# First layer of batches 4 to 7 in block form, eleven long spin products, no zero fills, a split last PSUM bank, and a new order of all the work

## The chip, the core and the metric

The kernel runs on one core of one Trainium2 chip. The metric is device time in microseconds, from launch to end. The engines are named as the profile names them: PE (matrix products), PEld (its weight loads), DVE and ACT (elementwise work), POOL and SP (here mostly queues that issue transfers); "PEq", "SPq" and so on are an engine's instruction queue.

## What is computed

Attention without softmax, with a squared ReLU, and behind it a two-layer network with an exact GELU. From the reference:

```
scores = scale * np.matmul(q, k.transpose(0, 1, 3, 2))
attn = np.maximum(scores, 0.0) ** 2 / S
out = np.matmul(attn, v)
...
x = attn_out.transpose(0, 2, 1, 3).reshape(B * S, H * D)
h = x @ w_in
g = 0.5 * h * (1.0 + erf(h * inv_sqrt2))
return (g @ w_out).astype(np.float32)
```

q, k and v are 8 batches x 12 heads x 448 positions x 64, w_in is 768 x 2048, w_out is 2048 x 768, all in float32; the products are made in bf16. The output has 3584 rows of 768.

## The kernel before, in words

**Attention.** A batch has three head groups of four heads. A score tile (`add_steps`, L718) is one block of keys of one head group: four products on quarters of PE (L736), a ReLU out of PSUM on ACT (L748) or DVE (L750), a square on DVE (L757). Seven tiles make a head group; then 28 products make its values (`add_av`, L782, L797), which ACT and DVE copy out as xT (L515, L513). Batch 0 works in halves of 224 columns. Scores and values need q and k transposed. For batches 0 and 1 PE does that (`add_tk`, `add_tq`, L607, L635), with the identity that POOL makes (L1321). For batches 2 to 7 DMA transposes do it, issued by SP (`add_T_dma`, L662), three for each head group.

**First layer.** The plain form (`add_f1`, L838) makes one of 16 output tiles of a batch with six products of 448 columns (L849) and a GELU on ACT (L859). The block form (`add_blocks`, L935, `add_block`, L982) splits the weights and the columns of a batch into 2 x 2 blocks and makes the four results from seven block products instead of eight, after Strassen and Winograd: each block product is made of products of 224 columns (L993), 168 of them in a batch. It needs four sums of x (L960), sums of the weights that are made once (`add_wsums`, L918), and it passes its partial results through DVE (additions, L1030) and ACT (copies, L515; GELUs, L1039 and L1046). Before, batches 0 to 4 take the plain form and 5 to 7 the block form. The results stand in a ring of two batches (`h_ring`, L711), so the GELUs of batch b wait until the second layer has read batch b - 2.

**Second layer.** Rows go in 14 groups of 256 (group 0 as two plain tiles, `add_plain`, L1253). A group (`add_group`, L1130) is the same seven-product form: p1, p6, p2, p7, p5, p4, p3, each of eight products of 384 columns (L1166). Its sums of h are made by DVE (L1147), partial results are added by DVE (L1200) or copied (L513, L515), and SP stores the rows (L1127). Products p5 and p3 share the PSUM bank "c". In the last group (13) p3 and the addition behind it are made in a part of 256 columns and one of 128, in that same bank.

**Buffers.** PSUM has three tiles of two banks, "w" (scores, values, block products, the spin), and two single banks, "f" (everything else). Natural q and k have one buffer from batch 2 on, and their transposes two.

**What sets the order.** A planner (`Scheduler`, L182) holds all operations in the order in which the code adds them, 1436 in all. The text `ORDER` (L83) then fixes by hand what is issued when: each word is a letter for the engine (P for PE, A for ACT, D for DVE, G for POOL, S for SP) and the number of an operation in that list; `place` (L353) takes the words one by one. An engine runs its words strictly in that order. Words with Z are zero fills (L1493, L1499): products of zeros of so many columns on PE, whose result nobody reads. There are eight, all in the first four lines of the text. POOL's loads wait in its queue behind gates (`add_gate`, L698, L703): small copies that read a transposed q, so that a load doesn't overwrite what a transpose still reads. Before all that PE runs 45 spin products of 128 columns on zeros (L1333).

Some words, decoded by counting the additions: G0, G1, G3, G4 load k and q (first half) of batch 0's groups 1 and 2, G2 the values of group 0, G7 the second halves of q; G1435 makes the identity; S541 to S543 are the transposes of batch 4's first head group and P600 to P618 its score products; S704 to S706 are those of batch 5's first head group, whose score products begin at P763. In the new text numbers above some 740 shift: the identity is G1469, and batch 5's first score product is P783.

## Time and profile before

Three runs took 370.45, 370.65 and 370.81 us. The profile is of one execution; its page gives its span, from the first to the last instruction, and no time of its own for it.

| | us |
|---|---|
| median of three runs | 370.65 |
| span of the profiled execution | 367.9 |
| median less span (what lies around it) | 2.75 |
| PE busy, 3573 products | 359.3 |
| DVE busy | 285.1 |
| ACT busy | 199.4 |
| POOL busy | 62.9 |

The stages, by the busy time of each engine in stretches of the span (the ends are starts of products on PE):

| stretch, us | what PE does | PE | DVE | ACT |
|---|---|---|---|---|
| 0 to 34.75 | spin, batch 0's attention, its first layer begins | 31.42 | 27.53 | 28.21 |
| 34.75 to 82.04 | batches 0 to 2: attention, first layer of 0 and 1 | 47.29 | 31.82 | 26.84 |
| 82.04 to 145.57 | attention 2 to 4, first layer of 2, groups 1 to 3 | 63.00 | 54.61 | 36.45 |
| 145.57 to 220.47 | attention 4 to 6, first layer of 3, groups 3 to 5 | 74.90 | 64.71 | 50.65 |
| 220.47 to 250.06 | attention 6 and 7, first layer of 4, group 6 | 29.41 | 27.00 | 22.51 |
| 250.06 to 354.08 | block form of 5 to 7, groups 7 to 12 | 103.95 | 74.27 | 34.73 |
| 354.08 to 367.9 | group 13 and the last stores | 9.28 | 5.19 | 0.00 |

To read the profile's lines: a group line names the line of code, engine, operation, what is written and read, and the busy time; a timeline line gives the start, the duration and the number of merged instructions, and in brackets how long the engine sat idle before and what ended that. Products are pipelined: their durations overlap, so what one costs is read from the distance of starts. Times of transfers are from issue to landing.

### The profile page before, as it was taken

The numbers are of one execution on the slowest core, as the hardware profiler recorded it, in microseconds if no ns is written. First come the engines' busy times: TensorE is split into PE (matmuls) and PEld (weight loads), VectorE is DVE, ScalarE is ACT, GpSimd is POOL, SyncE is SP. The second block draws the span as 40 slices with busy tenths as digits, with TensorE's granted clock in tenths as the row PEclk, the third lists the DMA queues.
The fourth block names the chain that finished last, engine by engine and source line by source line (L and its number), as shares of the span: only waits on it lengthen the run. The fifth ranks groups of instructions, "written<-read, shape, count | busy, mean of one in ns | idle before, by whom it ended". The sixth has DMA issues, their size and how long they took to land.

```text
span 367.9 us, 8474 instructions
## 1 busy us (share of the span) xinstructions
PE 359.3 (98%) x3573; PEld 222.5 (60%) x3573; DVE 285.1 (78%) x473; ACT 199.4 (54%) x319; POOL 62.9 (17%) x103
## 2 busy tenths in 40 slices
PE   7999999999999999999999999999999999999995
PEld 6675654455544455544555544557876897688663
DVE  4998854699788889989598997998788558665862
ACT  5998954536367546765777568863540353045200
POOL 8766304230112140240302000000000000000000
PEclk9999999999999999999999999999999999999998
DMA  9999999999999999999999980002002301210233
GB/s 180 191 202 204 201 178 167 196 201 178 162 218 214 154 186 193 237 214 154 166 110 131 215 183 2 2 2 86 3 0 87 88 0 52 86 37 2 86 87 86
DMA packets 89542, 47.27 MB, mean 128 GB/s; under 512 B 55329, under 2 KB 86049, under 8 KB 89505
## 3 DMA queue, kind: packets, MB, share of 16 engines
q0 software_dynamic: 32912, 22.47, 43.8%
q1 hardware_dynamic: 55952, 23.76, 34.9%
q8 instruction: 28, 0.46, 0.5%
q10 hardware_dynamic: 640, 0.51, 0.4%
q14 instruction: 10, 0.07, 0.1%
HBM read 45.61 MB, written 11.01 MB: 154 GB/s over the span
## 4 chain that ended last, share of the span: by engine, by line
PE 78%; DMA 8%; SPq 5%; DVE 5%; issue 1%; POOL 1%; ACT 1%; DVEq 0%; POOLq 0%; ACTq 0%
PE pso L1166 30%; PE psh L849 19%; PE pb L993 13%; PE ps L736 8%; PE pav L797 7%; SPq L662 5%; DMA wout_sb<-in_moe_w_out_dram 4%; DVE a_sq L757 2%; DMA nq<-in_q_dram 1%; DVE t_sb L1103 1%; DMA qT<-nq 1%; DMA out_dram<-osb 1%; ACT a_sq L748 1%; PE tp L635 1%; DVE part L1030 1%
## 5 line engine op out<-in xcount | busy, mean ns | idle before, releaser
L748 ACT ACTIVATE a_sq<-ps 128x896 bf16<-128x896 f32 (+1 forms) x119 | 104.3, 918 | 36.8 <-PE ps L736 36.6
L757 DVE TENSOR_TENSOR a_sq<-a_sq 128x896 bf16<-128x896 bf16 (+1 forms) x169 | 97.0, 617 | 9.4 <-ACT a_sq L748 8.8
L849 PE MATMUL psh<-xT,win_sb 128*128 128x448 bf16 (+1 forms) x516 | 96.4, 340 | 0.4 <-issue 0.4
L849 PEld LDWEIGHTS <-win_sb 128*128 128x128 bf16 x516 | 48.1, 98 | 45.8 <-issue 9.7
L750 DVE TENSOR_SCALAR a_sq<-ps 128x896 bf16<-128x896 f32 (+1 forms) x50 | 53.5, 1078 | 17.1 <-PE ps L736 17.0
L859 ACT ACTIVATE h_sb<-psh 128x448 bf16<-128x448 f32 x80 | 43.2, 548 | 29.9 <-PE psh L849 29.6
L1166 PEld LDWEIGHTS <-s_sb 128*128 128x128 bf16 x424 | 40.7, 98 | 26.6 <-issue 2.0
L1030 DVE TENSOR_TENSOR part<-pb,part 128x448 f32<-128x448 f32 x60 | 34.6, 620 | 21.5 <-PE pb L993 21.5
L736 PE MATMUL ps<-qT,kT 64*64 64x448 bf16 (+1 forms) x756 | 47.9, 336 | 0.5 <-ACT a_sq L748 0.2
L1166 PEld LDWEIGHTS <-h_sb 128*128 128x128 bf16 x312 | 29.6, 98 | 22.5 <-issue 4.4
L1166 PE MATMUL pso<-wout_sb,s_sb 128*128 128x384 bf16 (+2 forms) x216 | 38.1, 320 | 0.1
L1166 PE MATMUL pso<-wout_sb,h_sb 128*128 128x384 bf16 x208 | 38.1, 326 | 0.0
L1166 PE MATMUL pso<-t_sb,s_sb 128*128 128x384 bf16 x208 | 38.1, 326 | 0.0
L797 PE MATMUL pav<-a_sq,v_sb 64*64 64x448 bf16 (+1 forms) x756 | 36.5, 329 | 0.3 <-issue 0.2
L736 PEld LDWEIGHTS <-kT 64*64 64x64 bf16 x756 | 18.5, 105 | 22.9 <-issue 17.1
L1039 ACT ACTIVATE h_sb<-part 128x448 bf16<-128x448 f32 x36 | 20.1, 578 | 20.2 <-DVE part L1030 19.9
L1200 DVE TENSOR_TENSOR osb<-pso,p_sb 128x384 f32<-128x384 f32 x39 | 21.7, 556 | 11.0 <-PE pso L1166 6.7
L993 PEld LDWEIGHTS <-win_sb 128*128 128x128 bf16 x288 | 27.6, 98 | 2.3 <-issue 0.4
L797 PEld LDWEIGHTS <-v_sb 64*64 64x64 bf16 x756 | 21.2, 107 | 11.7 <-issue 1.3
L703 POOL COPY gate<-qT 128x16 bf16<-128x16 bf16 x15 | 3.7, 246 | 111.0 <-DMA qT<-nq 111.0
L993 PEld LDWEIGHTS <-ws 128*128 128x128 bf16 x216 | 20.7, 98 | 0.0
L1147 DVE TENSOR_TENSOR s_sb<-h_sb 128x1024 bf16<-128x1024 bf16 x26 | 17.8, 685 | 2.3 <-PE pso L1166 2.3
(61 smaller groups left out, 298.4 us busy)
## 6 DMA issues: line engine op xcount, KB each, us to landing
nk<-in_k_dram POOLq DMA_DIRECT2D x23, 224.0 KB, 5.6
nq<-in_q_dram POOLq DMA_DIRECT2D x21, 224.0 KB, 8.3
v_sb<-in_v_dram POOLq DMA_DIRECT2D x5, 672.0 KB, 13.9
out_dram<-osb SPq DMA_DIRECT2D x8, 336.0 KB, 2.9
v_sb<-in_v_dram POOLq DMA_DIRECT2D x9, 224.0 KB, 8.6
out_dram<-osb SPq DMA_DIRECT2D x7, 288.0 KB, 3.2
out_dram<-osb SPq DMA_DIRECT2D x8, 240.0 KB, 3.0
win_sb<-in_moe_w_in_dram POOLq DMA_DIRECT2D x8, 192.0 KB, 8.6
```

Of the source, the lines that this page charges most:

```text
L736: nc.tensor.matmul(ps[64 * j : 64 * j + 64, e, x * w : x * w + w], kT[r, g, i * 128 + 64 * j : i * 128 + 64 * j + 64], moving, start=True, ...
L748: A.activation(ar, ps, AF.Relu, scale=c_att)
L750: V.tensor_scalar(ar, ps, c_att, 0.0, op0=mybir.AluOpType.mult, op1=mybir.AluOpType.max,)
L757: V.tensor_mul(box["a2"][:, :, :used], ar, ar)
L797: nc.tensor.matmul(pav[0][o2 : o2 + 64, e, :w], vt[b][r, 2 * g + e, bass.ts(i, D)], box["a2"][r, y, o : o + w], start=(i == 0), stop=(i == ...
L849: nc.tensor.matmul(ph[:, x * n : x * n + n], win_sb[:, kd, bass.ts(m + x, 128)], xT[b][:, kd, c], start=(kd == 0), stop=(kd == KD - 1),)
L859: A.activation(h_ring()[:, m : m + nm, o + c.start : o + c.stop], box[0][:, :S].rearrange("p (x n) -> p x n", x=nm), AF.Gelu,)
L993: nc.tensor.matmul(bank[name][:, y, z * HS : z * HS + HS], w[:, k, bass.ts(mm, 128)], right()[:, k], start=first and k == 0 and z == 0, st ...
L1030: V.tensor_add(get(to), ps(name), get(other))
L1039: A.activation(h_ring()[:, m : m + 2, o + half[c].start : o + half[c].stop], src().rearrange("p (x n) -> p x n", x=2), AF.Gelu,)
L1166: nc.tensor.matmul(box[bank][:, n0:n1], left()[:, kf], right()[:, kf, n0:n1], start=bool(need) and kf == 0, stop=kf == K2 - 1, skip_group_ ...
L1200: V.tensor_add(out()[:, n0:n1], box[bank][:, n0:n1], other()[:, n0:n1])
```

## The change

The block form starts at batch 4 (`NBLK = 4`): 16 plain first-layer tiles go, 28 block products come, with their sums, passes and GELUs; the buffers of the x sums, and what these sums wait for, shift by one batch. The spin is 11 products of 512 columns. The zero fills are gone. In group 13 the second part of p5 and of p3 (128 columns) goes to a bank of its own, "d", taken from the "w" tiles, and the first addition behind p5 is split as well. Group 6 moves one batch earlier in the code that adds operations, which only matters for numbers, since `ORDER` is new as a whole: it has 1470 words, and stretches of one kind of work, loads, transposes, gates and stores all stand elsewhere. The text below is cut; what is said of the order is counted from the whole of both texts.

```diff
@@ -50,6 +50,7 @@
 DMA_LAT = 2.13
 SWITCH = 0.11
 LEAD = 8
+NBLK = 4
 HALF_M = 6
 PASS_BIAS = -0.4
 SUM_BIAS = -0.3
@@ -77,91 +78,92 @@
 
 COLD_END = 0.0
 K_CUT = 4
-SPIN = 45
+SPIN = 11
 
 
 ORDER = """
-G0 G1 G2 G3 G1435 G4 G5 G6 A10 P11 D13 A16 P17 G7 D12 P14 D18 P42 P39 G8 P19 A15 P21 D43 P33 P36 D44
-A40 D20 Z128 A22 P54 G9 P25 P23 A37 D34 P51 D26 P48 A55 Z1056 D35 A24 P69 D56 Z1024 D41 A49
-P57 Z992 D38 A52 P63 Z448 G117 D70 P45 A58 D53 P66 A64 D50 P27 A46 G118 P31 D59 P60 D28 A67
-G119 D32 A47 P78 P29 D65 G120 A61 P81 Z1088 D68 D30 A79 P93 D62 P108 Z544 D71 A82 P84 Z992
-G121 A94 P75 D109 P72 G122 D83 A85 P90 P129 D80 G123 D73 A76 P105 A74 P102 D95 G124 P131 D130
-A91 P141 D86 A106 D77 P111 P96 D132 A103 P165 P143 D92 A112 D104 D107 A97 P156 D113 P87 G125
-D98 A166 P99 D110 G126 D88 A157 P114 A142 D100 A89 P174 G127 A101 P168 D115 P133 A144 P135
-A116 G128 D175 P171 P159 A169 D134 P251 D136 D170 A160 P145 D158 A172 D167 A252 P162 P186 D176
...
-S541 A465 P467 D462 A518 P470 G413 S542 P519 A516 G414 A459 G415 P521 D471 S543 G416 D472 A520
...
-P654 P594 D653 A646 D659 A655 D650 P596 A647 D667 S710 D595 P660 P766 P663 P672 D597 A661 D767
...
-P1391 D1386 D1390 P1393 D1392 P1395 D1394 P1397 D1405 D1396 P1399 D1403 D1398 S1401 P1407
-D1404 D1400 S1402 P1409 D1406 D1408 P1411 D1410 P1413 D1412 S1423 P1415 D1414 P1417 D1416
-P1419 D1418 S1424 P1420 D1421 S1425 D1422 S1426
+G3 G4 G0 G1 G7 G1469 G122 A10 P11 D13 A16 G117 P17 D12 P14 D18 G2 P42 P23 D15 P25 G6 A43 P36 P33
+P39 G5 D24 P21 D26 P19 G121 A37 P69 D34 P66 G118 A40 D20 D22 P57 A70 P51 G9 D35 P29 P27 A67 D38
+P48 D30 P135 D44 A58 P54 D41 D28 A52 P63 P129 D136 A49 P90 P31 G8 D55 A64 P78 P45 D50 A91 D68
+P96 D32 D46 A79 P93 D47 P105 A97 D53 P81 D59 A94 G120 P111 D56 A106 D71 P75 D65 A82 P72 D98 A112
+P60 D95 A130 D107 G124 P131 D73 A76 D61 P102 A74 P84 A62 D80 P143 D113 D132 A85 G119 P159 D83
+P156 P141 A103 G125 D77 D86 A157 D92 P108 P99 D104 A160 P162 A144 P133 D109 P87 D100 G126 A163
...
+P497 S541 P494 D563 A520 P517 D472 A498 D493 S549 P511 D481 A495 D469 A504 P488 D502 P482 A512
+S546 D489 P615 P618 P521 S547 A483 A518 D484 P535 A619 S544 D616 A522 P606 D496 P600 P609 S545
...
+P660 D622 P566 D565 A623 S704 D659 A661 D656 P630 P666 P568 A628 S389 D567 D638 S707 A631 D635
+P570 A667 D626 A569 S710 D632 P783 D629 P798 P645 D662 S711 D668 A784 D571 P795 P572 S709 D582
...
+P1413 A1362 D1412 A1368 A1402 P1415 A1385 D1414 A1382 P1417 A1357 A1365 D1416 A1348 P1419 D1423
+D1418 P1427 D1424 D1420 S1422 P1429 D1425 S1421 D1428 P1431 D1430 P1433 D1432 P1435 D1434 P1437
+D1426 D1436 P1439 D1443 D1444 D1438 P1456 S1441 P1447 D1440 S1442 D1445 P1449 D1448 P1451 D1446
+D1450 P1453 D1452 S1465 P1455 D1454 P1459 D1457 D1458 P1461 D1460 S1466 P1462 D1463 S1467 D1464
+S1468
 """
 
 
@@ -932,6 +934,8 @@
             s3 = one(3, m0, sub, part(0, 0), part(0, 1), [s1] + done)
             WS[m0] = {1: s1, 2: s2, 3: s3, 4: s4}
 
+    first_blocks = []
+
     def add_blocks(b):
 
 
@@ -946,13 +950,15 @@
         def t(n):
             def fn():
                 if "t" not in box:
-                    tag = "qT" if b == B - 1 else "kT"
+                    tag = "qT" if b == B - 2 else "kT"
                     box["t"] = tpool.tile([128, 4, K1, HS], BF16, tag=tag, name="xs")
                 return box["t"][:, n - 1]
 
             return fn
 
-        gone = [o for (bb, *_), o in QK.items() if bb == (B - 2 if b == B - 3 else B - 1)]
+        gone = [o for (bb, *_), o in QK.items() if bb == (B - 2 if b == B - NBLK else B - 1)]
+        if b == B - 1:
+            gone += first_blocks
 
         def xsum(n, op, l, r, deps):
             return sch.add(
@@ -974,6 +980,8 @@
                 todo.append(add_block(b, m4, y, ms, bank, x, t, TS, xs, old, half))
             for p in zip(*todo):
                 atoms += [(0.58, o) for o in p]
+                if b == B - NBLK:
+                    first_blocks.extend(p)
             for name in ("a", "b", "c"):
                 u, v = bank["end", name]
                 u.joint, v.joint = [v], [u]
@@ -1160,7 +1168,9 @@
 
         def product(bank, left, right, deps, need=(), frees=(), joint=(), n0=0, n1=ND):
             def fn(e):
-                if need:
+                if need and bank == "d":
+                    box[bank] = w_pp.tile([128, 2, NB], F32, tag="w", name="psd")[:, 0]
+                elif need:
                     box[bank] = f_pp.tile([128, NB], F32, tag="f", name="pso")
                 for kf in range(K2):
                     nc.tensor.matmul(
@@ -1220,33 +1230,49 @@
         c11 = passed("a", part(0, left), None, [p2, v2], frees=("f",))
         p7 = product("b", lambda: box["s", 3], lambda: tsum(3), [v2, s3], frees=("s3",))
         v3 = passed("b", part(1, right), first, [p7], need=("osb",))
-        p5 = product("c", lambda: box["s", 1], lambda: tsum(1), [s1, s2], need=("f",), frees=("s1",))
-        c22 = passed("c", part(1, right), part(1, right), [v3, p5])
+        ends = [("c", 0, ND)] if g < NG - 1 else [("c", 0, LAST), ("d", LAST, ND)]
+        p5 = [
+            product(
+                x, lambda: box["s", 1], lambda: tsum(1), [s1, s2],
+                need=("f",) if x == "c" else ("w",), n0=n0, n1=n1,
+            )
+            for x, n0, n1 in ends
+        ]
+        p5[-1].frees = ("s1",)
+        c22 = [
+            passed(x, part(1, right), part(1, right), [v3, o], n0=n0, n1=n1)
+            for o, (x, n0, n1) in zip(p5, ends)
+        ]
         p4 = product("b", lambda: h(1, o2), lambda: tsum(4), [v3])
         c21 = passed("b", part(1, left), first, [p4, v3], frees=("f", "p"))
-        ends = [(0, ND)] if g < NG - 1 else [(0, LAST), (LAST, ND)]
         p3 = [
-            product("c", lambda: box["s", 4], lambda: quad[1, 1], [c22, s4], n0=n0, n1=n1)
-            for n0, n1 in ends
+            product(x, lambda: box["s", 4], lambda: quad[1, 1], [o, s4], n0=n0, n1=n1)
+            for o, (x, n0, n1) in zip(c22, ends)
         ]
         p3[-1].frees = ("s4",)
         c12 = [
-            passed("c", part(0, right), part(0, right), [o], n0=n0, n1=n1)
-            for o, (n0, n1) in zip(p3, ends)
+            passed(x, part(0, right), part(0, right), [o], n0=n0, n1=n1)
+            for o, (x, n0, n1) in zip(p3, ends)
         ]
-        c12[-1].frees = ("f",)
+        c12[0].frees = ("f",)
+        if g == NG - 1:
+            c12[1].frees = ("w",)
         if g < NG - 1:
-            sch.add((("SP", 0.6, 2.8),), store(1, full, [nc.sync] * 2), [c22, c21], frees=("osb",))
+            sch.add((("SP", 0.6, 2.8),), store(1, full, [nc.sync] * 2), c22 + [c21], frees=("osb",))
             sch.add((("SP", 0.6, 2.8),), store(0, full, [nc.sync] * 2), [c11] + c12, frees=("osb",))
         else:
             sch.add((("SP", 0.6, 2.8),), store(0, left, [nc.sync] * 2), [c11])
-            sch.add((("SP", 0.6, 2.8),), store(1, full, [nc.sync] * 2), [c22, c21])
-            for o, (n0, n1) in zip(c12, ends):
+            sch.add((("SP", 0.6, 2.8),), store(1, full, [nc.sync] * 2), c22 + [c21])
+            for o, (_, n0, n1) in zip(c12, ends):
                 c = slice(ND + n0, ND + n1)
                 sch.add((("SP", 0.6, 2.8),), store(0, c, [nc.scalar, nc.sync]), [o])
         for bb in bs:
             readers.setdefault(bb, []).extend(mine)
-        return [(1.3, o) for o in (p1, p6, p2, p7, p5, p4)] + [(1.3 / len(p3), o) for o in p3]
+        split = 1.3 / len(ends)
+        return (
+            [(1.3, o) for o in (p1, p6, p2, p7)] + [(split, o) for o in p5] + [(1.3, p4)]
+            + [(split, o) for o in p3]
+        )
 
     plain = []
 
@@ -1329,8 +1355,9 @@
     A.activation(warm, warm, AF.Gelu)
 
     spin = w_pp.tile([128, 2, NB], F32, tag="w", name="spin")
+    zeros = zero[:, :1].to_broadcast([128, NB])
     for _ in range(SPIN):
-        nc.tensor.matmul(spin[:, 0, :128], zero, zero, start=True, stop=True)
+        nc.tensor.matmul(spin[:, 0, :], zero, zeros, start=True, stop=True)
     ctx.enter_context(tc.manual_schedule())
 
 
@@ -1426,8 +1453,8 @@
         add_load(3, g, g + 1)
     add_v(3, 0, G)
     flow, plans = [], {}
-    F1B = {2: 1, 3: 2, 4: 3, 5: 4}
-    GROUPS = {2: (1,), 3: (2, 3), 4: (4, 5), 5: (6,)}
+    F1B = {2: 1, 3: 2, 4: 3}
+    GROUPS = {2: (1,), 3: (2, 3), 4: (4, 5, 6)}
     for b in range(2, B):
         add_steps(steps(b), dve=True)
         if b == 2:
@@ -1448,7 +1475,7 @@
                     add_load(b + 2, g, g + 1)
                 add_v(b + 2, 0, G)
         flow += [y for g in GROUPS.get(b, ()) for y in add_group(g)]
-    add_wsums(at(B - 1, 1), [F1[B - 4, m, None] for m in range(KF)])
+    add_wsums(at(B - 1, 1), [F1[B - NBLK - 1, m, None] for m in range(KF)])
 
     def woven(x, y):
 
@@ -1460,7 +1487,8 @@
                 out.append(y.pop(0))
         return out + y
 
-    end = woven(add_blocks(B - 3), add_group(7))
+    end = add_blocks(B - 4)
+    end += woven(add_blocks(B - 3), add_group(7))
     end += add_group(8)
     end += woven(add_blocks(B - 2), add_group(9))
     g10 = add_group(10)
```

## The prediction

> **What bounds the kernel now.** I read the page first: which engine is busy, and where.
>
> ```profile
> span 367.9 us, 8474 instructions
> PE 359.3 (98%) x3573; PEld 222.5 (60%) x3573; DVE 285.1 (78%) x473; ACT 199.4 (54%) x319; POOL 62.9 (17%) x103
> PE   7999999999999999999999999999999999999995
> DVE  4998854699788889989598997998788558665862
> DMA  9999999999999999999999980002002301210233
> PE 78%; DMA 8%; SPq 5%; DVE 5%; issue 1%; POOL 1%; ACT 1%; DVEq 0%; POOLq 0%; ACTq 0%
> ```
>
> PE is busy in every slice but the first and last, and it carries 78% of the chain that ended last. A busy PE need not be a PE at work, though, so I went to PE's timeline for what each product costs when nothing holds it: the distance from one start to the next (columns: start, modelled duration).
>
> ```profile
> 53.11 6.98 PE L849 MATMUL psh<-xT,win_sb 128*128 128x448 bf16 x36
> 60.02 0.76 PE L736 MATMUL ps<-qT,kT 64*64 64x448 bf16 x12
> 60.72 3.58 PE L849 MATMUL psh<-xT,win_sb 128*128 128x448 bf16 x18
> 64.23 0.76 PE L736 MATMUL ps<-qT,kT 64*64 64x448 bf16 x12
> ...
> 259.30 1.31 PE L993 MATMUL pb<-xs,win_sb 128*128 128x224 bf16 x12
> 260.45 1.31 PE L993 MATMUL pb<-xT,ws 128*128 128x224 bf16 x12
> 261.60 1.31 PE L993 MATMUL pb<-xT,win_sb 128*128 128x224 bf16 x12
> ```
>
> 36 first-layer products take 60.02-53.11 = 6.91 us, 18 take 64.23-60.72 = 3.51. So one costs (6.91-3.51)/18 = 0.189 us, and 0.11 is left over each time that PE turns from attention to dense products. A block product of 224 columns costs 1.15/12 = 0.0958 us. In the same way three score steps take 0.70 (60.02 to 60.72), and eleven steps of scores and values take 2.21 (111.04 to 113.25): 0.189 a step, and 0.13 for the turn. A second-layer product costs 0.1625 (357.98 to 359.28, eight of them).
>
> With these prices I added up the old order, word by word, and laid the sum beside the timeline. The last product ends at 352.0 in the sum and about 363.4 in the profile. Of the 11.4 us between, 9.6 are there by 34.75 (batch 0's ninth first-layer tile, m = 8): 5.2 before the first transpose, the rest waits of the start, where DVE and ACT are full. In the 329 us after it only 1.8 us are waits: about 0.6 near 99, 0.3 near 102, 0.4 near 250, 0.45 near 275. So after the start PE is the bound, and **PE's sum is the forecast's backbone**.
>
> **The change, part by part.** Sums are made against the profiled execution's span of 367.9 us. The page has no own time for that execution; the median of the runs, 370.65, is 2.75 us longer, and I carry that over.
>
> *Block form of batch 4.* Removed: 96 products x 0.189 = 18.14 us. Added: 168 x 0.0958 = 16.09. **-2.05 us**. [...] The rows above, each product with its own load, show 0.0958, so I go by them.
> DVE gets 20 additions and 4 sums more: from runs of four back to back (2.31 us) and the sums at about 0.45, 20 x 0.58 + 4 x 0.45 = 13.4 us. They lie in the block stage, beside PE: at 250.06 to 354.08 DVE was busy 74 of 104 us (71%). ACT trades 16 GELUs for 16 GELUs and 4 copies.
>
> *The new order.* Counting stretches of one kind on PE (transposes, attention, dense), the old list has 110 and the new one 121: 11 x 0.11 = **+1.2 us**. From batch 0's tile m = 8 to the last product the new list comes to 326.4 us by these prices, the old one to 326.9: most of the block form's gain goes into turns.
>
> *Zero fills.* 6272 columns; at 0.0958 per 224 columns 2.7 us. All lie between 8.46 and 20, where ACT and DVE are full (11 to 20: nearly 9 of 9 us each), so PE waits there anyway: **0**. If the fills did hold up score products, -2.7. If a less busy PE slows, the start's product work between 8 and 20, some 6 us, doubles within 12 us: at most +1.3. The granted clock can't settle it: it says 1.00 even where 45 spin products of 128 columns take 3.8 us (5760 columns, 0.15 us per 224). [...] The longest wait of PE after the spin was 0.86 us (for a load, before 9.72), and fills are 0.2 to 0.6 us each.
>
> *Eleven long products.* 5632 columns against 5760, at the pace of the old ones 3.7 us against 3.8. The first transpose waits for ACT's cast until 5.20 in any case: 0, between -0.1 and +0.2.
>
> *Order of the start.* The identity now stands behind five POOL loads instead of four. One issue is 0.72 to 0.92, so it ends near 5.5 instead of 4.61 and the first transpose starts 0.3 to 0.45 later. Against that, the ACT and DVE work listed ahead of batch 0's tile m = 8, by its rows, sums to 50.3 us on two engines instead of 51.8: -0.7. I take **-0.3**; ends -1.5 and +1.
>
> *Split last bank.* Old tail:
>
> ```profile
> 361.88 1.48 PE L1166 MATMUL pso<-wout_sb,s_sb 128*128 128x256 bf16 x16
> 363.40 0.62 DVE L1200 TENSOR_TENSOR osb<-pso,osb 128x256 f32<-128x256 f32 x2 [0.76 <-PE pso L1166]
> ```
>
> Both additions start after both products, since they share a bank. With two banks the 256-column addition (0.42) runs beside the 128-column product. Eight of these take about 0.55 us of the 1.48, so the first store issues 0.5 earlier and the second behind it. Splitting another product costs 0.02 (1.48 against 1.46). The 128-column half of that product now opens the last group and needs two sums; DVE has 2.6 us for four operations of 0.5 to 0.68, so up to 0.2 late. **-0.5**.
>
> *Moved loads and GELUs.* Batch 0's first value load moves from third to eighth among POOL's loads. By the issue sizes 2.4 MB then land up to and with it; at 183 GB/s to 10 us and 190 after, that is 13 us plus a landing tail of 1 or 2. Its value product moves from behind 10 score tiles (13.74) to behind 12 (about 16): nothing, with about 1 us to spare. At the end batch 7's block form now runs ahead of groups 9 and 10, which still read the ring slot of batch 5, so its 16 GELUs must wait for group 10's last product. From four in 2.26 us and two in 0.98 they take about 8.8 us; PE has one block product and group 11 in between, 9.7 us. Again nothing; without that spare 0.9, group 12 and all behind it would wait, up to 1 us.
>
> *Waits.* The four old ones (1.8 us) stand at places that are all rearranged: -1.8. New ones are unknown: from 0 to the 4.2 of the first rival and 2.4 of the second. I take +1.5, close to what the old order had over the same length.
>
> Sum: -2.05 + 1.2 - 0.3 - 0.5 - 1.8 + 1.5 = -1.95; span 365.95, time **368.7 us** (367.4 to 369.8 if this case holds).
>
> **Rivals.**
> *Transposes come late (slower).* The columns are issue line and microseconds to landing:
>
> ```profile
> qT<-nq SPq DMA_TRANSPOSE x36, 6.4
> kT<-nk SPq DMA_TRANSPOSE x18, 6.8
> ```
>
> Counted in PE work by the prices above, in the old list between 6.9 and 23 us stand between the last transpose of a head group and its first score product, mostly 13 to 18. In the new list it is 6 to 8 for most, 4.4 for batch 4's first group and 4.6 for batch 5's. Against a landing of 6.4 to 6.8 that is a wait of 2.0 to 2.4 on PE at two places, with dense work queued behind the waiting product. Each transpose also waits for a load, which waits in POOL's queue for a gate on earlier transposes: POOL spent 111 us at gates, so lateness is handed on from batch to batch, and all transfers must fit a stage about 17 us shorter. It decides once the waits pass 2 us: with 4.2 in the two places and 1.5 more at batches 6 and 7 the time is 368.7 + 4.2 = **372.9**. Against it: the old order's 6.9 at batch 2 cost PE nothing, and SP often issued up to 5 us before its place in the list.
>
> *DVE becomes the bound of the attention stage (no change).* With 18 us of dense work gone from beside attention, DVE has, from batch 3's first value product to batch 7's second, about 104 us of rows in 117 of PE (89%); the old list 109 in 130 (84%). If DVE manages only 87%, it needs 119.7: 2.4 more, **371.1**. Against it: the old stretch from 220.47 to 250.06 held DVE busy for 27.00 of 29.59 (91%), with about 0.4 of wait.
>
> *The start shrinks by more (faster).* If fills and early waits were in PE's way, up to 2.7 go, and with few new waits the time is 368.7 - 2.2 = **366.5**.
>
> **How the numbers follow.** Forecast 0.47, start shrinks 0.18, DVE bound 0.12, late transposes 0.23. The range leaves out the worst of the late transposes and the best of the start: 366.5 to 372.8. About 0.2% (0.74 us) is what a measurement of this kernel can tell from no change. Faster takes forecast and start (0.65), less 0.02 for its upper edge: 0.63. No change: 0.12; slower: 0.25, with part of the DVE case.
>
> **What the next profile would show.** Block rows for batch 4 at 0.096 each, before the last value product; batch 0's tile m = 8 by 34.5; no PE wait above 0.5 us after it; the last two additions apart, the first beside PE. I am wrong if score products of batches 4 and 5 wait for a transpose, if PE's starts in the attention stage stand further apart than the prices, or if spin, transposes and scores before 20 us run slower than now.

## The result and the profile after

The changed kernel takes **380.63 us** (378.06 to 383.24), the one before 370.55 (369.39 to 370.81) beside it: a ratio of 1.028 [1.0245, 1.0318], slower. The forecast was 368.7, in a range from 366.5 to 372.8, so both the size and the sign were wrong. The profiled execution took 381.77 us; its span is 380.0, 12.1 longer than before.

The page of the changed kernel, the lines that answer to those of before:

```profile
span 380.0 us, 8571 instructions
PE 362.2 (95%) x3603; PEld 228.0 (60%) x3603; DVE 297.1 (78%) x506; ACT 197.3 (52%) x315; POOL 64.1 (17%) x103
PE   8799998999999989999996999999999999999995
DVE  3989966468879779999785699998997765877673
PEclk9989999899999999999999699999999999999999
DMA  9999999999999999999999821000100023032233
PE 61%; DMA 17%; SPq 13%; ACT 3%; DVE 3%; issue 2%; POOL 1%; POOLq 0%; DVEq 0%; ACTq 0%
```

PE's share of the chain has fallen from 78% to 61%, and what took its place is transfers (DMA) and SP's queue, from which the transposes are issued. PE's row shows holes at the seventh slice (57 to 66.5 us) and at the twenty-second (199.5 to 209), and the granted clock (PEclk) falls in the slices beside them. PE's timeline at the two holes, with the wait and its releaser in brackets:

```profile
64.41 0.38 PE L738 MATMUL ps<-qT,kT 64*64 64x448 bf16 x4
67.39 0.57 PE L738 MATMUL ps<-qT,kT 64*64 64x448 bf16 x8 [2.60 <-DMA qT<-nq]
67.89 2.00 PE L851 MATMUL psh<-xT,win_sb 128*128 128x448 bf16 x6
69.83 0.96 PE L738 MATMUL ps<-qT,kT 64*64 64x448 bf16 x8
...
203.73 1.46 PE L1176 MATMUL pso<-wout_sb,s_sb 128*128 128x384 bf16 x8
209.56 0.96 PE L738 MATMUL ps<-qT,kT 64*64 64x448 bf16 x8 [4.36 <-DMA qT<-nq]
```

At 67.39 a score tile of batch 2's second head group waits for a transpose of q that SP issued at 57.08 and that landed at about 67.25. At 209.56 batch 7's first score product waits in the same way. The six first-layer products from 67.89 stand for 1.94 us instead of the 1.23 that their price gives: behind the wait PE runs at half its clock (granted 0.50 from 68.36 to 71.77). PE's waits by releaser (total us, times, longest):

```profile
PE ps L738 <- DMA qT<-nq: 7.0, 2, 4.4
...
PE pav L799 <- DMA v_sb<-in_v_dram: 1.0, 1, 1.0
...
PE ps L738 <- DMA kT<-nk: 0.6, 1, 0.6
PE pso L1176 <- DVE osb L1210: 0.5, 1, 0.5
```

The table lays the prediction's own sum beside this trace, word by word, as was done for before. The lag is how far PE's start of a product stands behind the sum of the prices ahead of it.

| product | start, us | lag, us | what came since the row above |
|---|---|---|---|
| batch 0's tile m = 8 | 34.48 | 12.4 | the start (before: 9.6 at 34.75, with 2.7 of fills in its sum) |
| first score tile of that head group of batch 2 | 64.41 | 12.5 | |
| 5 us behind the wait | 72.50 | 16.9 | wait 2.60, and 1.7 at half clock |
| in attention 3 to 4 | 108.87 | 17.5 | wait 0.52 for DVE |
| in attention 4 | 141.45 | 18.7 | wait 0.99 for a load of v |
| in attention 6 | 178.49 | 19.4 | wait 0.57 for a transpose of k |
| batch 7's first score product | 209.56 | 23.9 | wait 4.36 |
| 8 us behind it | 217.15 | 26.6 | 2.7 at half clock |
| the last products | 374 | 26.85 | |

Behind tile m = 8 the lag grows by 14.4 us, where before it grew by 1.8. The whole difference of the spans comes out of three numbers: PE's work 348.54 instead of 351.99 (-3.45, of which 2.7 are fills that the old start hid), the lag at tile m = 8 (+2.8, the same fills), and what comes behind it (+12.7): 12.05 of 12.1. From 217.15 to the end, block stage included, PE is on pace within 0.3 us in 157.

The transposes land faster than before in the median (us from issue to landing; before 6.4 and 6.8), while the loads of k take 10.0 instead of 5.6:

```profile
qT<-nq SPq DMA_TRANSPOSE x36, 4.6
kT<-nk SPq DMA_TRANSPOSE x18, 4.4
nk<-in_k_dram POOLq DMA_DIRECT2D x23, 224.0 KB, 10.0
```

The median hides the two that PE waited for. Batch 2's took 10.2 us to land, and the three of batch 7's first head group took 6.9 to 11.9 (before 6.4 to 8.7). Those of batch 7 also had to wait for loads that went out late. POOL's timeline shows it, first in the changed kernel, then before (columns: start, duration, in brackets the wait):

```profile
181.16 0.48 POOL L705 COPY gate<-qT 128x16 bf16<-128x16 bf16 x2 [18.97 <-DMA qT<-nq]
...
190.59 0.21 POOL L705 COPY gate<-qT 128x16 bf16<-128x16 bf16 x1 [7.30 <-DMA qT<-nq]
191.08 0.70 POOL L471 DMA_DIRECT2D nq<-in_q_dram  x1 [0.28 <-issue]
191.77 1.42 POOL L550 DMA_DIRECT2D nk<-in_k_dram  x2
```

```profile
177.67 0.21 POOL L703 COPY gate<-qT 128x16 bf16<-128x16 bf16 x1 [14.08 <-DMA qT<-nq]
178.21 0.70 POOL L548 DMA_DIRECT2D nk<-in_k_dram  x1 [0.33 <-issue]
178.90 0.73 POOL L469 DMA_DIRECT2D nq<-in_q_dram  x1
```

The loads of batch 7's first head group stand behind a gate of another head group now and go out at 191, 13 us later than before. SP's transposes follow, in the changed kernel and before:

```profile
198.29 4.28 SPq L664 DMA_TRANSPOSE kT<-nk  x1
202.62 5.64 SPq L664 DMA_TRANSPOSE qT<-nq  x2
```

```profile
197.18 2.57 SPq L662 DMA_TRANSPOSE kT<-nk  x1
200.98 5.61 SPq L662 DMA_TRANSPOSE qT<-nq  x2
```

They are issued within 1.7 us of one another, and the last one that the group needs (from 202.62 and, before, from 203.71) lands at 209.5 instead of 210.1. What has moved is the reader: before, PE came to batch 7's first score product at 220.47; now it stands there at 205.2, its earlier waits included.

### The profile page after: what moved, and what is told of

Same layout as the page of the kernel before. It is cut to its first block, busy times and chain, and to the rows that moved or that the text cites. A ratio compares the mean times of both kernels' runs of the same rounds, so it can differ in the third digit from the quotient of the medians.

```text
span 380.0 us, 8571 instructions
## 1 busy us (share of the span) xinstructions
PE 362.2 (95%) x3603; PEld 228.0 (60%) x3603; DVE 297.1 (78%) x506; ACT 197.3 (52%) x315; POOL 64.1 (17%) x103
## 3 DMA queue, kind: packets, MB, share of 16 engines
HBM read 45.61 MB, written 11.01 MB: 149 GB/s over the span
## 4 chain that ended last, share of the span: by engine, by line
PE 61%; DMA 17%; SPq 13%; ACT 3%; DVE 3%; issue 2%; POOL 1%; POOLq 0%; DVEq 0%; ACTq 0%
PE pso L1176 26%; PE pb L1001 17%; SPq L664 13%; DMA qT<-nq 10%; PE pav L799 6%; PE ps L738 5%; PE psh L851 5%; DMA nq<-in_q_dram 4%; ACT a_sq L750 3%; DMA v_sb<-in_v_dram 3%; PE spin L1360 1%; DVE a_sq L752 1%; DVE osb L1210 1%; DMA out_dram<-osb 1%; SPq L1135 1%
## 5 line engine op out<-in xcount | busy, mean ns | idle before, releaser
L750 ACT ACTIVATE a_sq<-ps 128x896 bf16<-128x896 f32 (+1 forms) x124 | 107.9, 917 | 44.5 <-PE ps L738 43.1
L851 PE MATMUL psh<-xT,win_sb 128*128 128x448 bf16 (+1 forms) x420 | 78.7, 339 | 0.0
L752 DVE TENSOR_SCALAR a_sq<-ps 128x896 bf16<-128x896 f32 x45 | 48.7, 1087 | 24.1 <-PE ps L738 21.4
L851 PEld LDWEIGHTS <-win_sb 128*128 128x128 bf16 x420 | 38.6, 98 | 37.4 <-issue 10.3
L1038 DVE TENSOR_TENSOR part<-pb,part 128x448 f32<-128x448 f32 x80 | 46.8, 619 | 13.3 <-PE pb L1001 10.0
L1047 ACT ACTIVATE h_sb<-part 128x448 bf16<-128x448 f32 x48 | 24.9, 573 | 44.6 <-DVE part L1038 18.1
L861 ACT ACTIVATE h_sb<-psh 128x448 bf16<-128x448 f32 x64 | 34.8, 551 | 23.2 <-PE psh L851 22.9
L1176 PE MATMUL pso<-t_sb,s_sb 128*128 128x384 bf16 (+1 forms) x208 | 38.3, 328 | 0.0
L1176 PE MATMUL pso<-wout_sb,s_sb 128*128 128x384 bf16 (+1 forms) x208 | 37.7, 324 | 0.0
L1001 PEld LDWEIGHTS <-ws 128*128 128x128 bf16 x288 | 27.7, 98 | 1.3
L1001 PE MATMUL pb<-xT,win_sb 128*128 128x224 bf16 x192 | 22.3, 259 | 0.0
```

The costliest lines, as they stand in the source:

```text
L750: A.activation(ar, ps, AF.Relu, scale=c_att)
L752: V.tensor_scalar(ar, ps, c_att, 0.0, op0=mybir.AluOpType.mult, op1=mybir.AluOpType.max,)
L851: nc.tensor.matmul(ph[:, x * n : x * n + n], win_sb[:, kd, bass.ts(m + x, 128)], xT[b][:, kd, c], start=(kd == 0), stop=(kd == KD - 1),)
L861: A.activation(h_ring()[:, m : m + nm, o + c.start : o + c.stop], box[0][:, :S].rearrange("p (x n) -> p x n", x=nm), AF.Gelu,)
L1001: nc.tensor.matmul(bank[name][:, y, z * HS : z * HS + HS], w[:, k, bass.ts(mm, 128)], right()[:, k], start=first and k == 0 and z == 0, st ...
L1038: V.tensor_add(get(to), ps(name), get(other))
```

## The experiments

"Before" below is always the kernel before on the same chip: 370.15 for e1 to e4, 369.59 for t1 to t3 and f4, 370.11 for t4, h2, h12 and b11, 370.31 for k1 and s1. The theories: **A**, the order of gates and loads on POOL makes the waits; **B**, PE's idle time halves its clock (0.50 is granted behind the waits of 2.60 and 4.36 us), and that is a loss of its own; **C**, lateness is handed on from batch to batch; **D**, a transpose comes late just because SP issues it last of nine. (In e1's text the clock is called A, and B is any other reason.) Later: **E**, transfers are the bound of the attention stage, and PE now comes to its end too early; **F**, the plain first-layer tiles were the cover of that stage; **G**, the block form is worth its 2 us and only the new order loses.

### The two waits: clock, and the order of loads

e1 fills the two waits with zero products, so that PE isn't idle:

```diff
-... D296 P342 P312 G269 ...
+... D296 P342 Z5120 P312 G269 ...
-... D909 D927 P964 D732 S954 ...
+... D909 D927 D732 Z7680 P964 S954 ...
```

> The changed kernel with zero products put into its two long waits: 5120 columns ahead of the score product that waited 2.60 us for batch 2's last transpose, 7680 columns ahead of the one that waited 4.36 us for batch 7's. Transposes and loads stand as they are, so the waits themselves should stay. Theory A (the wait costs twice: its own length, and then the clock of 0.50 that PE is granted behind it): the granted clock stays at 1.00 at both places, the 1.7 and 2.7 us by which the products behind the waits ran late come back, and 380.6 becomes about 376.3. Theory B (the products behind the waits ran late for another reason, operands or a busy DMA): nothing changes, 380.6.

Measured: 381.94 (378.08 to 383.23), 1.029 [1.0231, 1.035]. Its profile did what the theory of the clock says. PE's timeline at the first wait:

```profile
64.62 2.33 PE L1527 MATMUL fill<-zero 64*64 64x512 bf16 x10
67.44 0.57 PE L738 MATMUL ps<-qT,kT 64*64 64x448 bf16 x8 [0.49 <-DMA qT<-nq]
67.95 1.31 PE L851 MATMUL psh<-xT,win_sb 128*128 128x448 bf16 x6
```

The products behind it are back at 1.23 a six (67.95 to 69.18), and batch 7's first score product starts at 208.09, 1.5 earlier, with full clock behind it. The profiled run is 378.08 with a span of 376.3, 3.7 less than the changed kernel's profiled one. But the changed kernel's four runs hold one of 378.06 too, and the medians show no gain. So the clock step is there in the trace and can be taken away; that it is worth 4 us of the median is not shown.

e2 moves batch 7's first loads of q and k ahead of the gate, e3 does the like for batch 2 (a load of v ahead, two loads of batch 3's q and two of the second layer's weights behind), e4 does both:

```diff
-... D833 P898 G870 A679 P880 G866 ... G865 ... G868 ...
+... D833 P898 G866 G865 G868 G870 A679 P880 ...
```

```diff
-... S232 G242 G270 D286 P362 ... G149 ... G274 ... G239 ... G238 A328 G240 ...
+... S232 G242 G149 D286 P362 ... A328 G240 G270 G274 G239 G238 ...
```

> The changed kernel with three loads of batch 7 (q of group 0, k of groups 0 and 1) moved in POOL's queue ahead of the third gate of batch 6, which they do not need. Theory A (batch 7's wait comes from loads queued behind a gate of another head group): these loads issue 8 to 9 us earlier (182 to 185 instead of 191 to 194), the 4.36 us wait goes, and the 2.7 us of slow clock behind it with it: 380.6 becomes about 373.6. Theory C (lateness is handed on from batch to batch, all transfers being too slow for a shorter stage): the transposes are held up elsewhere, and less than 2 us come back, 379 or more.

> The changed kernel with two q loads of batch 3 and the first two loads of the second layer's weights moved in POOL's queue behind the last gate of batch 2, so that they do not run beside batch 2's last transpose. Theory A (this transpose took 10.2 us to land because 1.9 MB of loads were in flight beside it): it lands in 5 to 7 us, the 2.60 us wait and the 1.7 us of slow clock behind it go: 380.6 becomes about 376.3. Theory D (it comes late because SP issues it last of nine): the wait stays, 380 to 381.

> The edits of the two load runs together, no zero products. Theory A: both waits and both stretches of slow clock go, 7.0 + 4.3 us, and 380.6 becomes about 369.3, 1.2 below the kernel before. Theory C (lateness handed on): one wait shows up again further on, 372 or more.

Measured: e2 376.74, 1.0167 [1.0136, 1.0199]; e3 386.49, 1.040 [1.0347, 1.0453]; e4 380.7, 1.0261 [1.0179, 1.0342]. e2 is the only order of loads that helped, by some 4 us, about half of what A asks, and hardly by earlier data for batch 7: they land 1.2 us earlier (208.3). At batch 7 a wait of 2.1 is left instead of 4.36, and the clock doesn't step. PE's waits in e2:

```profile
PE ps L738 <- DMA qT<-nq: 4.3, 2, 4.0
PE ps L738 <- DMA kT<-nk: 2.1, 1, 2.1
```

Batch 7's first score product starts at 209.56 in the changed kernel, 208.09 in e1, 208.37 in e2, 209.16 in e4 and 213.54 in e3. Its data land at 208 to 209.5 in all of these but e3, and a load that is issued earlier need not land earlier. The three loads that e2 and e4 move went out in e4 at 185.1 to 186.5 instead of 191.1 to 192.5, and landed at 195.5, 196.7 and 197.8 instead of 194.9, 196.0 and 198.2. In e3 A is right about the one transpose: it lands in 6.1 us instead of 10.2, and the wait of 2.60 is gone. But what was put behind came late in its turn: the second layer's weights (0.9), a transpose of k (3.2) and a partial result (3.6), and the time grew. D falls, A falls as the whole cause, and C fits e4 (372 or more) but not e2 (379 or more). This is what led to E.

### How many bytes the stage can carry

t1 leaves out the loads of v for batches 3 to 7 (3.4 of 47.3 MB) in the changed kernel and reads batch 2's v instead, t2 does so before; both leave that part of the computation out. t3 is the kernel before with each of these loads copied once more into a spare tensor in DRAM, 3.4 MB more. t4 is t1 with e4's order of loads.

```diff
+            if b > 2:
+                vt[b] = vt[2]
+                return
             get_v(b)
```

```diff
             nc.gpsimd.dma_start(vt[b][:, 2 * g0 : 2 * g1], kv_view(v, b, g0, g1))
+            if b > 2:
+                nc.gpsimd.dma_start(extra[b], v[b])
```

> The changed kernel without the value loads of batches 3 to 7 (five loads of 0.69 MB, 3.4 of the 47.3 MB that the DMA moves); the values of batch 2 are used instead, so the output is not the reference's. The order of all other work stands. Theory E (the DMA is the bound of the attention stage: it moves some 190 GB/s without a gap until batch 7's transposes land near 209 us, and PE now comes there with 24 us less work behind it): 3.4 MB at 190 GB/s are 18 us, the transposes land some 15 us earlier, before PE needs them; the waits and the slow clock behind them go, 380.6 becomes 367.5 to 370. Theory A (the order of gates and loads on POOL makes the waits): the gates stand where they stood, and most of the time stays, 377 to 381.

> The kernel before without the same five value loads (values of batch 2 used instead, so the output is not the reference's). Theory E: in this order PE reaches batch 7's first score product about 8 us after its transposes have landed, so fewer bytes give almost nothing: 369.2 to 370.3, under 1 us. If the old order was held up by the DMA as well, it gains several us.

> The kernel before with 3.4 MB more traffic: behind each value load of batches 3 to 7 the same values are copied once more into a tensor that nobody reads. Theory E: the DMA falls about 18 us behind over the stage, the old order's spare 8 us at batch 7 is used up, and PE waits for transposes: 370.2 becomes 378 to 383, with granted clocks of 0.50 behind the waits. Theory A (order, not traffic): the loads issue in the same order, 370 to 372.

> The changed kernel without the value loads of batches 3 to 7 (batch 2's values are used, so the output is not the reference's) and with the two load edits tried before: nothing else loads beside batch 2's last transpose, and batch 7's first loads stand ahead of the gate they do not need. Leaving the value loads out alone gave 375.0, with 5 us still lost at batch 2, where those loads have not begun. Theory E (the transfers are the bound of the attention stage): with fewer bytes and no collision at batch 2 hardly any wait is left, 369.5 to 371.5. Theory A (order of gates): no more than what the load edits gave with all bytes, 375 or more.

Measured: t1 375.01, 1.0114 [1.0049, 1.0179]; t2 369.0, 0.9971 [0.9945, 0.9998]; t3 402.18, 1.0848 [1.0769, 1.0927]; t4 373.68, 1.0094 [1.0062, 1.0126]. The same 3.4 MB less bring the changed kernel 5.6 us back, with the loads moved 7.0, and before only 0.6. And 3.4 MB more cost before 32 us. (The copies of t3 are also written to DRAM, 14.45 MB instead of 11.01, so t3 is no exact mirror of t2.) PE's waits in t3, then in t1:

```profile
PE ps L737 <- DMA qT<-nq: 15.5, 3, 9.6
PE pso L1167 <- DVE osb L1201: 10.3, 1, 10.3
```

```profile
PE ps L741 <- DMA qT<-nq: 4.1, 2, 3.6
```

t3's waits for transposes are of the changed kernel's kind, at the kernel before's own order of work. The 10.3 are another: PE waits for DVE, and DVE had waited 11.7 us for a store that SP issued behind late transposes. In t1 the last transpose of batch 7's first group lands at 198.7 instead of 209.5 and batch 7 waits for nothing; the longest wait, 3.6, is the one at batch 2. What is left in t4, 3.5 us, has names in its trace: between 82 and 109 us PE waits 1.7 for a load of the second layer's weights, 1.2 for a load of batch 2's values, 0.6 for a transpose of q and 1.5 for DVE, which had waited for a store.

E's mechanism holds: fewer bytes take the waits away in the new order and change next to nothing in the old one, and more bytes bring such waits into the old one. Its sizes do not: it gave t1 367.5 to 370, t4 369.5 to 371.5 and t3 378 to 383. And the bytes are not shown to be all of it. Between 100 and 150 us the changed kernel's transfers moved 176 GB/s and before's 200. Whether the new order of loads makes them slower there, or PE's own delay, which frees their buffers later, no run separates.

### The block form in the old order, and a new order of the old work

k1 is the block form of batch 4 in before's order with before's fills: the 16 plain tiles are taken out from beside attention 6 and 7 and the block products put behind the last score products. (The spin and the split bank are the new ones as well.)

```diff
+NBLK = 4
-SPIN = 45
+SPIN = 11
-    F1B = {2: 1, 3: 2, 4: 3, 5: 4}
-    GROUPS = {2: (1,), 3: (2, 3), 4: (4, 5), 5: (6,)}
+    F1B = {2: 1, 3: 2, 4: 3}
+    GROUPS = {2: (1,), 3: (2, 3), 4: (4, 5, 6)}
...
-    end = woven(add_blocks(B - 3), add_group(7))
+    end = add_blocks(B - 4)
+    end += woven(add_blocks(B - 3), add_group(7))
```

> The block form of batch 4 alone, in the order of the kernel before: its 16 plain first-layer tiles, which stood beside the attention of batches 6 and 7, are taken out, and the block products follow the last score products, in the pattern that the old order has for batch 5; loads, gates, transposes and stores as before, zero fills kept (spin and last bank as in the change). Theory F (the plain tiles are the cover of the attention stage: 18 us of PE work that need neither a transfer nor DVE, and the block form has no such work): the stage from 205 to 245 us runs at the pace of ACT and DVE, PE waits there for them and, at batch 7's first products, up to 2 us for transposes; with the clock steps behind such waits 376 to 390. Theory G (the block form by itself is worth its 2 us and only the new order loses): 367.5 to 369.5.

Measured: 389.85 (388.52 to 393.8), 1.0534 [1.0482, 1.0586]: 19.5 us slower, and behind the start PE waits for no transfer. The stretch from 215 to 235 (columns: stretch, length, busy us of PE, PEld, DVE, ACT and POOL, granted clock, DMA share, GB/s) in k1, then before:

```profile
215.00:225.00 10.00, 5.96 (x63) 2.46 (x60) 8.90 (x16) 5.65 (x9) 0.00 (x0) 0.80 0.35 83
225.00:235.00 10.00, 8.82 (x63) 3.84 (x59) 10.00 (x16) 4.89 (x8) 0.00 (x0) 0.51 0.01 2
```

```profile
215.00:225.00 10.00, 10.00 (x95) 4.99 (x94) 8.01 (x14) 7.24 (x12) 0.00 (x0) 1.00 0.45 108
225.00:235.00 10.00, 10.00 (x97) 4.74 (x96) 8.80 (x12) 7.94 (x14) 0.00 (x0) 1.00 0.01 2
```

Before, the first-layer tiles stand between score tiles, and PE is full while DVE and ACT square the scores. Without them PE makes 63 products in 10 us instead of 95, goes to half clock, and DVE is full: the stage runs at DVE's and ACT's pace. F holds in that order: 16 plain tiles are 18.1 us of PE work that needs no transfer, no DVE and one GELU a tile, and that is what the stage lived on.

Two more kernels lay the work out anew with the transfers (loads, gates, transposes, stores) in before's order; the words of PE, DVE and ACT were chosen by the planner with a transpose set to 1.65 us (the author's setting, not a measured time). h12 is the changed kernel's code with fills, b11 before's. h2 is the changed kernel with 10 us of PE work of batch 6 and groups 4 and 5 put ahead of batch 7's first score product. Their first differences in PE's words:

```diff
 h12  -P23 P25 P36 P33 P39 P21 ...        +P39 P19 P21 P33 P36 P54 ...
 b11  -P253 P195 P180 P198 P137 P139 ...  +P180 P253 P195 P189 P198 P137 ...
 h2   -P964 D732 S954 P955 P919 ...       +D732 S954 P919 ... P943 ... P749 ... P964 P955 ...
```

> The changed kernel with 10 us of PE work that needs no transfer (the rest of batch 6's scores and values, the rest of group 4, the first products of group 5) moved ahead of batch 7's first score product; all loads, gates, transposes and stores as they were. Theory E (batch 7's data land near 209 us whatever PE does): the 4.36 us wait and the 2.7 us of slow clock go, and batch 7's score tiles, now closer together, cost up to 5 us on DVE and ACT: 374 to 379, with no wait for a transpose of batch 7. If the transposes are late because PE is late (it frees their buffers), the wait stays and the time is above 381.

> The changed kernel (block form from batch 4, long spin, split last bank) with the loads, gates, transposes and stores in the order of the kernel before, the zero fills back, and PE, DVE and ACT in an order searched for on the kernel's own planner, with a transpose counted as 1.65 us of the DMA's time instead of 1.0. PE's sum before batch 7's first score product is back near the old one. Theory E: no wait for transfers, and what is left of the block form is 2 us of PE against DVE, which the block form of batch 4 loads more: 367 to 371. If the block form itself makes the kernel slow: 374 or more.

> The kernel before, all instructions and the order of every load, gate, transpose and store as they were; PE, DVE and ACT from batch 0's ninth first-layer tile on in an order searched for in the same way. Theory E: the old order has 1.7 us of waits after the start, which can go, and 13 more turns of PE cost 1.4: 366 to 370. It shows what order alone is worth where the transfers are left in peace. If a searched order fares badly on the chip whatever the transfers do: 373 or more.

Measured: h2 380.43, 1.026 [1.0199, 1.0321]; h12 389.03, 1.0497 [1.0423, 1.0571]; b11 380.32, 1.0265 [1.0199, 1.0331]. h2 lost the wait at batch 7, as E asks, and gained nothing (E gave 374 to 379): batch 7's score tiles now stand closer together, and the lag grows from 22.1 to 26.1 us while DVE and ACT catch up (between 220 and 235 us PE waits for them seven times, 3.0 us in all). h12 waits for no transfer from 34 to 218 us. It loses behind that: its block products wait 13 times for DVE's additions, 10.5 us in all, and b11's 6 times, 4.8 us, the first at 264.65. E's times for both (367 to 371, 366 to 370) were far off. So G is not shown: no order here made the block form of batch 4 pay. And b11, the very instructions of before, is as slow as the changed kernel: an order alone is worth 10 us in this program, here without any wait for a transfer behind the start.

### Two parts alone

f4 is before without the eight zero fills; s1 is before with the split last bank only.

```diff
-G0 G1 G2 G3 G1435 ... D20 Z128 A22 ... A55 Z1056 D35 ... D56 Z1024 D41 A49 ...
+G0 G1 G2 G3 G1427 ... D20 A22 ... A55 D35 ... D56 D41 A49 ...
```

```diff
+        ends = [("c", 0, ND)] if g < NG - 1 else [("c", 0, LAST), ("d", LAST, ND)]
-... S1423 P1415 D1414 P1417 D1416 P1419 D1418 S1424 P1420 D1421 S1425 D1422 S1426
+... S1425 P1415 P1416 D1414 P1419 D1417 D1418 P1421 D1420 S1426 P1422 D1423 S1427 D1424 S1428
```

> The kernel before without its eight zero fills (6272 columns), all else as it was. The prediction took 0 for this. Theory B (a clock step costs: PE is 56% busy between 17.1 and 20.5 us without fills and is then granted 0.50 for 3.4 us): about 1.5 us of product work is late, 370.2 becomes 371 to 372. If ACT and DVE set the pace of the start in any case: 370.2. If the fills were in the way: 368 to 369.

> The split last PSUM bank alone, in the kernel before. The prediction took 0.5 off. The changed kernel's profile shows 5.92 us from the last group's p3 to the end of the span, against 6.02 in the old one, since the stores of the last rows stand in SP's queue behind one another; by that it is 0.1, and the two can't be told from each other or from no change by much: 369.6 to 370.2 beside 370.1.

Measured: f4 370.04, 1.0009 [0.9981, 1.0036]; s1 370.6 over 13 runs, 1.0002 [0.9979, 1.0025]. Neither can be told from no change. In f4 the granted clock was 0.50 from 11.9 to 18.7 us, and no loss of time can be told.

## Why the prediction was wrong

**The failing step is *Waits*:** "New ones are unknown: from 0 to the 4.2 of the first rival and 2.4 of the second. I take +1.5, close to what the old order had over the same length." They came to 14.4: 9.04 of waits that the trace names (2.60 + 0.52 + 0.99 + 0.57 + 4.36), 4.4 of half clock behind the two long ones, 1.0 small. The sum priced what PE does, and never set the moment at which PE asks for a batch against the moment at which its bytes can be there. Both could be read from before. PE's work ahead of batch 7's first score product is 209.8 us in the old list and 185.5 in the new one: 24.3 less, since dense work went behind it, while the bytes are the same. Counted in the traces, 42 first-layer products fewer are 7.9 us of it, 80 second-layer products 13.0, the fills 2.7: the block form takes the smaller part, the new order the larger. With the lag of 12.4 PE would be there at 198. In before's trace that group's last transpose landed at 210.1, while PE came at 220.47, so some 10 us were spare, and the new order spends 24 in their place. (Its transposes could have come earlier: their loads had landed by 191.9, and SP had waited 12.7 us at a store ahead of them.) Against the landing at 209.5 that is 11.5 us of delay, wherever in the stage it falls; with 2.7 of half clock behind it, 14.2 of the 14.4. t1 shows that the bytes decide when they land (198.7 instead of 209.5 with 3.4 MB less); that the new order of loads adds nothing of its own is not shown, and its lower rate from 100 to 150 us leaves it open.

**Rival 1, late transposes, was the mechanism and carried 0.23.** Its condition held ("all transfers must fit a stage about 17 us shorter"), but its places and price did not. It counted the PE work between a transpose's word and its reader against a landing of 6.4 to 6.8, and so looked to batches 4 and 5. The waits fell at batches 2 and 7: at batch 2 the landing took 10.2, at batch 7 the transposes stood behind loads that stood behind a gate. Its price, 4.2 and 1.5 more, was two fifths of the 14.4, with no term for the clock.

**Block form, -2.05.** As a price it was right; from PE's timeline in the changed kernel:

```profile
270.63 1.89 PE L1001 MATMUL pb<-xs,win_sb 128*128 128x224 bf16 x18
272.36 1.31 PE L1001 MATMUL pb<-xs,ws 128*128 128x224 bf16 x12
```

1.73 us for 18, 0.096 each, as said. What was missing is the other side of "removed: 96 products": they were cover, and DVE and the transfers were next. k1 puts a price on that in the old order, 19.5 us, where nothing was rearranged for it.

**Turns, +1.2:** borne out; the sum with them matches the trace within 0.3 us from 217 to the end. **Fills, 0:** right, f4 measured +0.45 [-0.7, +1.3]; that the clock would hold there no run shows: in f4 it was 0.50 from 11.9 to 18.7 us. **Spin, 0, and start, -0.3:** the spin runs from 1.00 to 5.88 instead of 0.99 to 4.98, outside the -0.1 to +0.2 named, but that is not its form: the same eleven products took 3.93 us in e1, and the 45 short ones 4.98 in b11. The first transpose starts at 5.80 (0.6 later, more than the 0.3 to 0.45 expected), and tile m = 8 at 34.48, 0.27 earlier and within the 34.5 named. **Moved loads and GELUs, 0:** right; neither place shows a wait.

**Split bank, -0.5:** too much. The additions come apart as described, the first beside PE:

```profile
374.96 0.61 PE L1176 MATMUL psd<-wout_sb,s_sb 128*128 128x128 bf16 x8
375.16 0.42 DVE L1210 TENSOR_TENSOR osb<-pso,osb 128x256 f32<-128x256 f32 x1 [0.32 <-PE pso L1176]
375.61 0.29 DVE L1210 TENSOR_TENSOR osb<-psd,osb 128x128 f32<-128x128 f32 x1
```

But from the start of p3 to the end of the span it is 5.92 us (374.08 to 380.0) instead of 6.02 (361.88 to 367.9): 0.1. The stores behind it, which I did not follow, take the rest; s1 shows none of it.

**Rival 2, DVE as bound:** not in the changed kernel, whose waits for DVE behind the start are 0.5 us. It comes next, though: k1 and h2 lose mainly around the attention of batch 7, waiting for ACT and DVE (7.0 us in k1 between 210 and 240 us, 3.0 in h2), h12 and b11 mainly in the block stage, waiting for DVE (10.5 and 4.8 us).

**What stays open.** Whether any order makes the block form of batch 4 pay; how much of the lateness is the bytes and how much the new order of loads; and how much of the median the clock costs. No kernel here was faster than before by more than the measurement shows, t2 apart, which leaves work out.

## What to carry to other kernels

Before taking dense work out of a stage that loads its operands, add up the engine's work ahead of each load-fed step, old and new, and lay it beside the landing times in the old trace: the old slack is a first measure of what may be spent, and here it was 10 us against 24. A stage in which no engine waits may still stand exactly at its transfers' pace; a run with a few per cent more bytes (+3.4 MB cost 32 us) or fewer (0.6) tells which side it is on. And the work that a cheaper form replaces may be the cover for three others (in k1 its going cost 19.5 us), so a price per instruction is the gain only where the engine stays full.

## What the runs showed of the hardware

In the changed kernel the granted clock fell to 0.50 after stretches in which PE was not idle throughout. Stretches of 3.41 us of its trace (columns as above):

```profile
17.08:20.50 3.42, 1.91 (x49) 1.05 (x45) 3.42 (x8) 3.42 (x6) 2.03 (x4) 1.00 1.43 195
20.50:23.90 3.40, 3.40 (x80) 2.92 (x75) 2.65 (x8) 2.27 (x5) 2.81 (x5) 0.51 1.36 200
...
64.95:68.36 3.41, 0.97 (x11) 0.46 (x12) 0.35 (x1) 1.35 (x2) 0.69 (x2) 1.00 1.30 197
68.36:71.77 3.41, 3.41 (x29) 1.31 (x31) 0.74 (x1) 2.12 (x4) 3.34 (x6) 0.50 1.32 206
...
204.93:208.34 3.41, 0.27 (x2) 0.00 (x0) 0.33 (x1) 0.00 (x0) 0.00 (x0) 1.00 0.80 211
208.34:211.75 3.41, 2.19 (x24) 1.28 (x28) 1.56 (x2) 0.92 (x1) 0.00 (x0) 0.50 1.05 244
211.75:215.17 3.42, 3.42 (x29) 1.55 (x22) 1.99 (x4) 1.62 (x3) 0.00 (x0) 0.50 1.03 199
```

The clock was 0.50 from 20.57 to 23.98, from 68.36 to 71.77 and from 208.31 to 215.13, so for 3.41, 3.41 and 6.82 us (and once more behind the last products, from 378.97); these three falls lie 47.79 and 139.95 us apart, 14 and 41 times 3.41 within 0.15. PE was busy for 28% of the 3.41 us before the fall at 68.36, for under 9% before that at 208.31 and for 56% before that at 20.57 (1.90 of 3.41). In this trace the clock came back each time behind 3.41 us in which PE was busy throughout; the stretch from 208.34, busy for 2.19 of 3.41, did not bring it. The busy share alone does not decide, though: in e2 PE waits 2.07 us ahead of 208.37, so 3.41 us that hold this wait are busy for 39% at most, and from 200 to 220 us the clock stayed at 1.00. In the changed kernel a wait of 2.60 us cost 1.7 more, one of 4.36 cost 2.7.

The prediction took 0 for a slower clock at the start, and it gave no wait a price in clock; the trace has half clock at the start too (20.57 to 23.98) and behind a wait of 2.60 us.
